# Products of x blocks 2 and 3 of the last block joined into one 128x4608 instruction, block 0's third spectra summed at once, and a new order

## Chip, cores and metric

One Trainium2 chip, one of its cores. The time is device microseconds of one launch. The kernel before has been timed three times: 206.28, 206.78 and 206.79 us, median 206.78.

## What is computed

Two independent results stand side by side in the output of 1 x 2048 x 1152 bfloat16 numbers. Cut to what matters:

```python
# A: local attention, 32 heads of 18, window of 8 keys at distance 0, 2, .. 14 behind the query
qkv = A_x @ A_wqkv                      # 2048x576 @ 576x1728
logits[s, w] = q[s] . k[s - 2*w] * 18**-0.5      # -1e9 where s - 2*w < 0
o[s] = sum_w softmax(logits)[s, w] * v[s - 2*w]
a = o @ A_wo                            # 2048x576 @ 576x576

# B: short convolution, product, long convolution, gate
k_shift = sum_t k[s - t] * shift_k[:, t]         # 4 taps
kv = k_shift * v
y = irfft(rfft(kv, 4096) * rfft(ssm_k, 4096))[:2048] + kv * ssm_D
b = q * y
out = concat(a, b)
```

## The kernel before, in words

**Work units.** The kernel is written as 361 small jobs with names. A table of names at the top, `ORDER`, is walked once at the end (L1103 before the change), and each job emits its instructions in that order to the five engines' queues. There is no scheduler behind it: each engine executes its own instructions in the order in which the table emits them, and semaphores hold an instruction until what it reads is there and what it overwrites has been read. So the table alone decides what stands behind what in each queue.

**Part A.** `q..`, `k..`, `v..` are the projections (L317 and L433, matmuls at L322, L326, L333 and, for the first pieces, L439): for example `k13a` and `k13b` are the two halves of tokens 1024 to 2047 of column group 3 of k, 8 matmuls of 512 columns and two small tails on TensorE, then one copy by ScalarE out of PSUM (L355). `Lhgc` multiplies q by shifted k (VectorE, L706), `Ghgc` sums the product over each head on TensorE (L720). `sm0a` to `sm0d` are the softmax of token half 0: maximum and difference on VectorE (L744 to L748), exponential on ScalarE (L752), sum on TensorE with logarithm and power on ScalarE (L763, L764), scaling on VectorE (L756). `D` spreads the weights over partitions by DMA, `V` multiplies them with v (VectorE, L813), `A` adds eight terms on TensorE (L824, L838), `O` is the output projection (L888, L880).

**Part B.** The tokens fall into four blocks of 512. `Ti` makes kv of block i from the taps on VectorE (L517, L520, L536). `Mi0` and `Mi1` fold kv (L545 on TensorE, two copies by ScalarE at L548). `xigh` transforms block i to spectra (L682, one copy at L684), three parts of 2304 numbers for each of 128 partitions, in the tile `xw`. `Fm` folds filter block m (L602, two copies at L605), `Kmcg` transforms it (L567 and L568, one copy at L618) into the tile `Ks`; eight `K` units for each of four blocks. The spectra are held as part 0, part 1 and their sum; the sum is the "third spectrum", so that a complex product takes three real ones. For blocks 2 and 3 the sum is made by DMA (`Tx`, `Tk`), for blocks 0 and 1 on VectorE: `ak` for the filter and `ax` for x (L942). `U` adds filter blocks by DMA. `RG0` to `RG4` are ScalarE copies that regroup the weights of v (L780).

**The products.** For output block j, third t of the columns and x block i, `pjti` multiplies three parts of the spectrum of x block i by that of filter block j-i, one VectorE instruction of 128x2304 (`spectral_product`, L950). `zjti` adds it into PSUM, 16 matmuls (L975), and the last i copies the result out by ScalarE (L988); for the last one, (3,2,3), half is copied by VectorE. In the last output block, j = 3, the products of x blocks 0 and 2 are subtracted first (`y3t0`, L958), so that only `z3t0`, `z3t1` and `z3t3` exist. `i` is the inverse transform (L1010), `b` folds back (L1059), `g` gates with q (L1075) and stores; `i3384L` and `g3384` are the same for the last 192 columns (L1029, L1038, L1020) and end the kernel.

**What holds a unit back.** PSUM is handed out as four tiles of two banks in turn (`banks`): a unit on TensorE that needs a tile waits until ScalarE has copied the unit that used it four tiles earlier. `M` and `F` take two tiles each, `K`, `x` and `G` groups one. A product is written to one of five homes (`PRODUCT`, by the list `PHOMES`); it waits until the `z` that read the home before has run. Homes 2 and 3 lie side by side in `qk`, 2304 numbers each.

Of the kernel before, what the change touches and what calls it, by code (L numbers as in the profile page):

```python
# [12 lines left out]
ALU = mybir.AluOpType  # L13
# [7 lines left out]
    T0 k03a' T1 S1 k03b I1 k02a k02b Lk2 Lv2 I0 k00a' Lk3 Lv3 M01 X5 k00b q10a Ex q10b Lf3 T2 Lo3 q13a' q13b  # L21
    k10a k10b T3 k13a' Lf2 k13b q12a q12b N2 Lo2 k01a M10 k01b Lf1 M00 k11a k11b q11a M11 q11b Lf0 N3 Lw SV L001
    k12a M20 k12b x001 M21 x021 q24a x020 q24b x000 Lo1 k24a Fr Lo0 Z2 N1 RG3 k24b RG2 F3 RG0 F2 L000 K310 G000
    K311 K210 K211 L002 K313 G001 RG4 F1 G002 L003 G003 K302 L004 G004 K301 L010 K212 L011 K303 K213 K203 N0 F0
    L012 K200 K300 G010 L013 K201 K312 K202 RG1 G011 G012 K113 K103 G013 L014 G014 K112 K102 K101 L100 K100 K010
    K111 K110 sm0a K001 K013 sm0b v24a' L101 v24b L102 G100 L103 G101 K012 sm0c sm0d U3 U2 K000 K011 K003 G102
    K002 D0 D1 v11a v11b G103 L104 G104 ak00 M30 v12a' v12b ak02 v01a ak01 L110 G110 M31 L111 G111 v01b v00a'
    L112 G112 L113 Wl v00b G113 x031 U1 L114 G114 V04 v10a' v10b A04 sm1a sm1b v02a v02b v03a' sm1c v03b x201
    V10 V11 sm1d V12 A10 v13a' v13b D2 x330 x310 x301 V13 A11 V20 V21 x200 x331 x230 x010 x221 A20 x321 V22 x210
    x011 V23 D3 V34 ax02 x220 x030 x300 D4 A21 V40 V41 A34 D5 O000' x211 V42 x320 x231 x111 x131 Tx2 A40 V43  # L30
    x120 x101 ax00 x130 ax01 V50 x121 x311 O001 A41 V51 O100' p000 x100 x110 O010 A50 V52 z000 O011' V53 O101
    A51 Tk2 p010 z010 ax10 O020' O021 p020 z020 O110' ak10 i000 p200 i02880 Q0 p100 z100 p101 p110 p111 Q1 z101
    i02881 i001 p121 p120 O111 z110 p201 z111 z120 p210 z121 O120 p211 z200 z210 z211 p212 z212 z201 p202 z202
    Tx3 p220 Tk3 p221 O030' p222 O121 b0288 z220 p301 z221 O031' p302 b00 z222 p303 i200 i100 g0 Q2 p300 y300
    p312 i12880 i201 i101 i12881 z300 z301 z303 p310 p311 y310 O130 b10 b1288 p313 g1 Q3 p322 O131' z310 p320
# [1100 lines left out]
```

## Time and profile before

| | us |
|---|---|
| median of three runs | 206.78 |
| the profiled execution | 206.3 |
| its span, first to last instruction | 204.6 |
| what lies around the span | 1.7 |
| busy: TensorE, VectorE, ScalarE | 196.9, 192.3, 155.6 |
| last product of the last block done on VectorE | 195.85 |
| last matmul issued | 199.6 |

A line of the timeline gives start, duration, engine, source line, operation, out<-in, the number of instructions merged, and in brackets how long the engine sat idle and who released it. PE is TensorE, PEld its weight load, DVE VectorE, ACT ScalarE. Instructions of one engine overlap a little: what counts for the rate is the distance from one start to the next, not the duration.

### The profile page before, as it was taken

The page shows a single profiled execution, that of the slowest core. Times are in us where ns is not written, and L with a number is a line of the kernel's source. Part 1 is how long each engine was busy: PE and PEld are TensorE (multiplying, and loading weights), DVE is VectorE, ACT ScalarE, POOL GpSimd, SP SyncE. Part 2 cuts the span into 40 slices and gives each one's busy share as a digit, 9 for nine tenths or more (in the row PEclk, how much of TensorE's full clock was granted, in tenths as well). Part 3 has the DMA queues.
Part 4 walks back from the last instruction along what each step waited for, and adds up shares of the span by engine and source line. Part 5 has one row for each costly group of instructions (what it writes and reads, how often), then busy time and mean ns, then how long its engine had stood idle before and what let it go on. Part 6 is the DMA issues. An engine that isn't in the chain of part 4 may idle for free.

```text
span 204.6 us, 5004 instructions
## 1 busy us (share of the span) xinstructions
PE 196.9 (96%) x2074; PEld 109.9 (54%) x2074; DVE 192.3 (94%) x146; ACT 155.6 (76%) x223; POOL 60.8 (30%) x106
## 2 busy tenths in 40 slices
PE   7999999999989999999999999999999999999990
PEld 2543544334455646543245556776666767766660
DVE  7559999999999999999999999999999999899992
ACT  4788995678899999966578678886778767767760
POOL 8989500011348581400380000004090001030300
PEclk9999999999999999999999999999999999999997
DMA  6999899989509869999899990879989303944555
GB/s 197 280 293 306 175 289 373 214 177 281 169 3 146 111 82 185 167 180 222 157 235 216 248 244 34 141 183 334 186 227 233 100 28 122 227 130 145 153 182 150
DMA packets 34916, 38.48 MB, mean 188 GB/s; under 512 B 17523, under 2 KB 28911, under 8 KB 34894
## 3 DMA queue, kind: packets, MB, share of 16 engines
q1 hardware_dynamic: 26668, 24.29, 46.5%
q0 software_dynamic: 5760, 11.36, 29.5%
q10 hardware_dynamic: 2466, 2.51, 3.6%
q8 instruction: 16, 0.26, 0.5%
q14 instruction: 6, 0.05, 0.1%
HBM read 13.11 MB, written 4.72 MB: 87 GB/s over the span
## 4 chain that ended last, share of the span: by engine, by line
PE 88%; DMA 3%; ACT 2%; DVE 2%; issue 1%; SPq 1%; DVEq 0%
PE ps_proj L322 18%; PE ps_fx L682 8%; PE ps_wo L888 8%; PE ps_z L975 8%; PE ps_inv L1010 7%; PE ps_acc L824 7%; PE ps_fk L567 5%; PE ps_log L720 5%; DMA Ks<-in_A_x_dram 3%; PE ps_proj L333 3%; PE ps_proj L326 3%; PE ps_proj L439 3%; PE ps_fk L568 3%; PE ps_fold L545 2%; PE ps_wo L880 1%
## 5 line engine op out<-in xcount | busy, mean ns | idle before, releaser
L322 PE MATMUL ps_proj<-xw 128*128 128x512 bf16 x160 | 38.5, 380 | 0.0
L706 DVE TENSOR_TENSOR av<-qk 128x4096 bf16<-128x4096 bf16 (+1 forms) x16 | 31.7, 2014 | 0.1
L322 PEld LDWEIGHTS <-xw 128*128 128x128 bf16 x160 | 13.9, 98 | 19.4 <-issue 5.7
L988 ACT ACTIVATE av<-ps_z 128x768 bf16<-128x768 f32 x23 | 17.2, 811 | 6.5 <-PE ps_z L975 6.0
L517 DVE TENSOR_TENSOR tB<-kj,skb 128x4608 bf16<-128x4608 bf16 (+1 forms) x8 | 19.3, 2416 | 0.1
L950 DVE TENSOR_TENSOR qk<-xw,Ks 128x2304 bf16<-128x2304 bf16 x14 | 18.9, 1354 | 0.3 <-PE ps_z L975 0.3
L684 ACT ACTIVATE xw<-ps_fx 128x576 bf16<-128x576 f32 x32 | 18.6, 665 | 0.3 <-PE ps_fx L682 0.2
L618 ACT ACTIVATE Ks<-ps_fk 128x576 bf16<-128x576 f32 x32 | 18.6, 699 | 0.2 <-PE ps_fk L568 0.2
L355 ACT ACTIVATE qk<-ps_proj 128x1024 bf16<-128x1024 f32 x14 | 14.3, 1023 | 5.2 <-PE ps_proj L333 2.8
L888 PE MATMUL ps_wo<-qk 128*128 128x288 bf16 x128 | 17.9, 287 | 0.0
L626 POOL DMA_DIRECT2D Ks<-Ks x8 | 10.1, 1426 | 26.0 <-PE ps_back L1059 19.3
L682 PE MATMUL ps_fx<-xw,TB 128*128 128x288 bf16 x128 | 17.7, 287 | 0.0
L567 PE MATMUL ps_fk<-Ks,TB 128*128 128x384 bf16 x62 | 16.5, 327 | 0.1
L824 PE MATMUL ps_acc<-av,ident 64*64 64x512 bf16 x160 | 15.3, 378 | 0.0
L1010 PE MATMUL ps_inv<-av,TI 128*128 128x288 bf16 (+1 forms) x112 | 15.2, 292 | 0.0
L568 PE MATMUL ps_fk<-Ks,TB 128*128 128x192 bf16 x62 | 15.2, 246 | 0.0
L682 PEld LDWEIGHTS <-TB 128*128 128x128 bf16 x128 | 11.9, 98 | 5.9 <-issue 2.7
L888 PEld LDWEIGHTS <-qk 128*128 128x128 bf16 x128 | 11.7, 98 | 5.4 <-issue 2.7
L355 ACT ACTIVATE v<-ps_proj 128x1024 bf16<-128x1024 f32 x9 | 9.3, 1033 | 6.5 <-PE ps_proj L322 4.5
L813 DVE TENSOR_TENSOR av<-Ks,v 128x4096 bf16<-128x4096 bf16 x6 | 13.5, 2286 | 0.0
L827 ACT ACTIVATE qk<-ps_acc 128x1024 bf16<-128x1024 f32 x8 | 8.2, 1024 | 6.7 <-PE ps_acc L824 6.7
L1010 PEld LDWEIGHTS <-TI 128*128 128x128 bf16 x112 | 10.6, 98 | 4.2 <-issue 1.1
(195 smaller groups left out, 441.6 us busy)
## 6 DMA issues: line engine op xcount, KB each, us to landing
Ks<-Ks POOLq DMA_DIRECT2D x8, 576.0 KB, 7.8
TB<-av SPq DMA_DIRECT2D x12, 256.0 KB, 5.4
kj<-in_B_k_dram SPq DMA_DIRECT2D x6, 504.0 KB, 7.0
vt<-in_B_v_dram SPq DMA_DIRECT2D x8, 288.0 KB, 5.3
Ks<-av SPq DMA_DIRECT2D x8, 256.0 KB, 5.6
out_dram<-qk ACTq DMA_DIRECT2D x5, 288.0 KB, 3.7
Ks<-in_A_x_dram SPq DMA_DIRECT2D x2, 576.0 KB, 5.4
xw<-in_A_wqkv_dram SPq DMA_DIRECT2D x2, 576.0 KB, 6.2
```

What stands on the lines that cost most here:

```text
L322: nc.tensor.matmul(ps[:, jp, :], wq(kb, comp, 128 * ct, 128), xT(kb, 1024 * jj + 512 * jp, 512), **se)
L355: nc.scalar.activation(view(t, o + pad + 1024 * jj, [[512, 2], [1, 512]]), ps[:], ACT.Copy)
L517: tt(to, view(kj, row * D, [[D, n], [D, 4], [1, D]]), view(skb, row * D, [[D, n], [0, 4], [1, D]]), ALU.mult)
L567: nc.tensor.matmul(o[:, 0:2], w, rhs[:, 0:2], start=start, stop=stop)
L568: nc.tensor.matmul(o[:, 2], w, rhs[:, 2], start=start, stop=stop)
L618: nc.scalar.activation(view(Ks, k_at(m, cs ^ (m & 1)) + 96 * gi, [[768, 3], [384, 2], [1, 96]]), acc3(ps), ACT.Copy, scale=(PSG, MSG)[cs][ ...
L682: nc.tensor.matmul(ps[:, pm, 0:HD], TX[:, 2 * pm + c, 128 * gi:128 * gi + 128], kv[:, 2 * c + pm, HD * h:HD * h + HD], start=(c == 0), sto ...
L706: tt(view(P, at, [[step, 4], [256, nj], [1, 256]]), view(t, o + 256 * hh, [[0, 4], [512, nj], [1, 256]]), view(tk, ok + 2 + 8 * ug + 256 * ...
L824: nc.tensor.matmul(acc[64 * o:64 * o + 64, h, :], ident[64 * h:64 * h + 64, 64 * h:64 * h + 64], view(P[s], 256 * u, [[2048, 2], [1, 256]] ...
L888: nc.tensor.matmul(ps[:, r, 0:HD], oT(hh, j + 2 * r, t)[:, o:o + 128], wo[:, t // 2, t % 2, HD * h:HD * h + HD], start=(t == 0 and not fli ...
L950: tt(product_home(n), view(xw, HB * XG[i] + QTR * t, [[HB, 3], [1, QTR]]), view(Ks, k_at(j - i, 0) + QTR * t, [[HB, 3], [1, QTR]]), ALU.mult)
L1010: nc.tensor.matmul(ps[:, c, 0:n], TI[:, sl, pm, 128 * c:128 * c + 128], Yall(j % 2, pm, sl, slice(c0, c0 + n)), start=(pm == 0 and sl == 0 ...
```

## The change

Three things change; the five engines do the same arithmetic.

1. For j = 3 the products of x blocks 2 and 3 become one instruction, `two_products`, of 128x4608, written over homes 2 and 3 at once. The three jobs `p303`, `p313`, `p323` go; `p302`, `p312`, `p322` do both.
2. The sums for block 0 (`ak00`, `ak01`, `ak02` and `ax00`, `ax01`, `ax02`, 128x768 each) become one `ak00` and one `ax00` of 128x2304.
3. `ORDER` is a new table throughout.

```diff
-    def third_sum(t, at, w):
+    def third_sum(t, at):
-        a, b, c = (view(t, at + HB * part, [[1, w]]) for part in range(3))
+        a, b, c = (view(t, at + HB * part, [[1, HB]]) for part in range(3))
         tt(c, a, b, ALU.add)
+    def two_products(n):
+        j, t, i = todo[n]
+        home, at = PRODUCT[PHOMES[n]]
+        assert (PHOMES[n], PHOMES[n + 1], XG[i + 1] - XG[i]) == (2, 3, 3)
+        tt(view(qk, at, [[HB, 2], [QTR, 3], [1, QTR]]), view(xw, HB * XG[i] + QTR * t, [[3 * HB, 2], [HB, 3], [1, QTR]]),
+           view(Ks, k_at(j - i, 0) + QTR * t, [[3 * HB, 2], [HB, 3], [1, QTR]]), ALU.mult)
...
     for n, (j, t, i) in enumerate(todo):
-        job(f"p{j}{t}{i}", spectral_product, n)
+        if (j, i) != (NBL - 1, 3):
+            job(f"p{j}{t}{i}", two_products if (j, i) == (NBL - 1, 2) else spectral_product, n)
...
-    for t in range(3):
-        job(f"ak0{t}", third_sum, Ks, k_at(0, 0) + QTR * t, QTR)
-        job(f"ax0{t}", third_sum, xw, HB * XG[0] + QTR * t, QTR)
-    job("ak10", third_sum, Ks, k_at(1, 0), HB)
-    job("ax10", third_sum, xw, HB * XG[1], HB)
+    for j in range(2):
+        job(f"ak{j}0", third_sum, Ks, k_at(j, 0))
+        job(f"ax{j}0", third_sum, xw, HB * XG[j])
```

Of the table, the two ends of block j = 3:

```diff
-    p311 y310 O130 b10 b1288 p313 g1 Q3 p322 O131' z310 p320 z311 p321 z313 ... y320 p323 ... g2 z320 z321 z323 b30 i3384L
+    p311 O131 i22880 y310 z310 z311 z313 i300 g1 p320 i22881 i301 Q3 p322 b2288 y320 z320 p321 z321 g2 z323 b30 i3384L
```

The queues of SyncE are the same instructions in the same order; on GpSimd one small DMA (L358) moves ahead of two memsets (L367, L369). The order is told at three places. The first is ScalarE's queue where the folds of kv end and the filter stage begins: L548 are the pairs of copies of `M`, L355 those of projections, L684 those of `x`, L780 the first `RG`. Before, from the copies of `M11` on:

```order
L548 ACTIVATE xw<-ps_fold 128x576 x2
L355 ACTIVATE qk<-ps_proj 128x1024
L548 ACTIVATE xw<-ps_fold 128x576 x2
L355 ACTIVATE qk<-ps_proj 128x1024
L684 ACTIVATE xw<-ps_fx 128x2x3x96
L548 ACTIVATE xw<-ps_fold 128x576 x2
L684 ACTIVATE xw<-ps_fx 128x2x3x96 x2
L355 ACTIVATE qk<-ps_proj 128x1024
L684 ACTIVATE xw<-ps_fx 128x2x3x96
L780 ACTIVATE xw<-Ks 128x576
```

The same place after, from the copies of `M10` on:

```order
L548 ACTIVATE xw<-ps_fold 128x576 x2
L684 ACTIVATE xw<-ps_fx 128x2x3x96
L548 ACTIVATE xw<-ps_fold 128x576 x6
L684 ACTIVATE xw<-ps_fx 128x2x3x96
L355 ACTIVATE qk<-ps_proj 128x1024
L684 ACTIVATE xw<-ps_fx 128x2x3x96
L780 ACTIVATE xw<-Ks 128x576
```

The pairs of `M11`, `M20` and `M21`, which had other copies between them, now follow each other, and one `x` unit (`x021`) has left this place for a later one.

The second place is the end of the filter stage in ScalarE's queue, from the last `G` of the first half of the logits (L724) to the next copy of v: L618 are `K` units, L752 is the exponential `sm0b`, L763 and L764 belong to `sm0c`. Before:

```order
L724 ACTIVATE av<-ps_log 128x1024
L618 ACTIVATE Ks<-ps_fk 128x6x96 x9
L752 ACTIVATE av<-av 128x2048
L355 ACTIVATE v<-ps_proj 128x1024
L618 ACTIVATE Ks<-ps_fk 128x6x96
L763 ACTIVATE av<-ps_tot 128x256
L764 ACTIVATE av<-av 128x256
L618 ACTIVATE Ks<-ps_fk 128x6x96 x4
```

After:

```order
L724 ACTIVATE av<-ps_log 128x1024
L618 ACTIVATE Ks<-ps_fk 128x6x96 x6
L752 ACTIVATE av<-av 128x2048
L618 ACTIVATE Ks<-ps_fk 128x6x96 x2
L355 ACTIVATE v<-ps_proj 128x1024
L618 ACTIVATE Ks<-ps_fk 128x6x96
L763 ACTIVATE av<-ps_tot 128x256
L764 ACTIVATE av<-av 128x256
L618 ACTIVATE Ks<-ps_fk 128x6x96 x6
```

The exponential stands three `K` units further ahead; of the 32 `K` units 18 stood ahead of this piece before, and 17 do now.

The third place is the end of VectorE's queue, from the gate of block 1 on: L950 and L958 are products of 2304, L953 the joined ones, the rows `av<-av,qk` the subtractions `y`, the rows `TB<-v,TB` the gates. Before:

```order
L1075 TENSOR_TENSOR TB<-v,TB 128x2304
L950 TENSOR_TENSOR qk<-xw,Ks 128x2304
L950 TENSOR_TENSOR av<-xw,Ks 128x2304
L950 TENSOR_TENSOR v<-xw,Ks 128x2304
L958 TENSOR_TENSOR av<-av,qk 128x2304
L950 TENSOR_TENSOR qk<-xw,Ks 128x2304
L1075 TENSOR_TENSOR TB<-v,TB 128x2304
L986 CAST av<-ps_z 128x4x192
```

These are the gate `g1`, then `p322`, `p320`, `p321`, `y320`, `p323`, the gate `g2` and the last copy. After:

```order
L1083 TENSOR_TENSOR TB<-v,TB 128x2304
L958 TENSOR_TENSOR av<-xw,Ks 128x2304
L953 TENSOR_TENSOR qk<-xw,Ks 128x4608
L966 TENSOR_TENSOR av<-av,qk 128x2304
L958 TENSOR_TENSOR v<-xw,Ks 128x2304
L1083 TENSOR_TENSOR TB<-v,TB 128x2304
L994 CAST av<-ps_z 128x4x192
```

The last product ahead of the end is now `p321` in place of `p323`, and the joined product stands ahead of the subtraction.

More of the change, by code (lines that the diff above doesn't have):

```diff
@@ L20 @@
 ORDER = """
[L21 to L35, printed above, removed]
@@ L37 @@
+    z300 z301 z303 p310 p312 b20 i12881 O130' b1288 p311 O131 i22880 y310 z310 z311 z313 i300 g1 p320 i22881
+    i301 Q3 p322 b2288 y320 z320 p321 z321 g2 z323 b30 i3384L g30 g3384
 """
```

15 lines of the change are left out of this document (14 added, 1 removed).

## The prediction

> **What bounds the kernel now.** I read the page first: the busy shares, and the chain of work that ended last, by engine.
>
> ```profile
> PE 196.9 (96%) x2074; PEld 109.9 (54%) x2074; DVE 192.3 (94%) x146; ACT 155.6 (76%) x223; POOL 60.8 (30%) x106
> PE 88%; DMA 3%; ACT 2%; DVE 2%; issue 1%; SPq 1%; DVEq 0%
> ```
>
> TensorE is busy 96% of the span and carries 88% of the chain; VectorE is close behind with 94%. No engine gets less arithmetic by this change. So only three things can move the end: TensorE's idle gaps, the time that it loses in passing from one kind of matmul to another, and VectorE or ScalarE running late enough to make new gaps. Where each engine is full is told by the windows (busy time of PE, PEld, DVE, ACT, POOL in each stretch, then the granted clock):
>
> ```profile
> 46.00:56.00 10.00, 10.00 (x82) 4.34 (x81) 9.72 (x9) 8.42 (x12) 2.52 (x6) 1.00 0.90 231
> 60.00:70.00 10.00, 9.59 (x93) 5.45 (x94) 10.00 (x6) 9.95 (x17) 8.63 (x9) 1.00 0.82 113
> 70.00:80.00 10.00, 10.00 (x100) 5.98 (x99) 9.86 (x11) 10.00 (x18) 5.48 (x5) 1.00 0.81 120
> 80.00:90.00 10.00, 10.00 (x91) 5.33 (x88) 10.00 (x7) 9.02 (x15) 2.38 (x2) 1.00 0.99 174
> 90.00:140.00 50.00, 50.00 (x543) 26.92 (x541) 49.78 (x32) 36.74 (x52) 6.42 (x9) 1.00 0.85 196
> ```
>
> From 60 to 80 us, the filter stage, ScalarE is as full as TensorE (9.95 and 10.00 of 10): it copies 32 `K` units out of PSUM, and TensorE can be no more than four PSUM tiles ahead of it. Before and after that stage ScalarE has room (8.42 of 10; 36.74 of 50). The granted clock is 1.00 in all of them, so I leave it out. Last, the waits of TensorE and of its weight loads (in total, times, longest):
>
> ```profile
> PE ps_log L720 <- DVE av L706: 0.6, 1, 0.6
> PE ps_z L975 <- DVE Ks L950: 0.2, 1, 0.2
> PEld L975 <- DVE av L958: 0.8, 3, 0.3
> ```
>
> Behind the start there is little to win: 0.6 at the first `G` (60.4 us) and 1.0 at the `z`.
>
> **The instructions that are joined.** VectorE loses seven instructions: three products and four sums. What one costs is the distance of starts, not the duration:
>
> ```profile
> 190.70 1.35 DVE L950 TENSOR_TENSOR av<-xw,Ks 128x2304 bf16<-128x2304 bf16 x1
> 191.97 1.35 DVE L950 TENSOR_TENSOR v<-xw,Ks 128x2304 bf16<-128x2304 bf16 x1
> 48.34 2.56 DVE L517 TENSOR_TENSOR tB<-kj,skb 128x4608 bf16<-128x4608 bf16 x1
> 50.93 2.75 DVE L520 TENSOR_TENSOR xw<-xw,tB 128x2304 bf16<-128x2304 bf16 x2
> 81.04 2.28 DVE L706 TENSOR_TENSOR v<-qk 128x4096 bf16<-128x4096 bf16 x1
> 83.24 2.28 DVE L706 TENSOR_TENSOR av<-qk 128x4096 bf16<-128x4096 bf16 x1
> L942 DVE TENSOR_TENSOR Ks<-Ks 128x768 bf16<-128x768 bf16 x3 | 1.5, 552 | 0.0
> L942 DVE TENSOR_TENSOR Ks<-Ks 128x2304 bf16<-128x2304 bf16 x1 | 1.4, 1352 | 0.0
> ```
>
> Two products of 2304 take 2 x 1.27 = 2.54 us. One of 4608 takes 2.59 by the tap products (48.34 to 50.93), and 2.20 x 4608/4096 = 2.48 by the logits: between 0.06 won and 0.05 lost, times three. I take nothing. Of the sums a duration exceeds the distance by 1.35 - 1.27 = 0.08, so three small ones take 3 x (0.552 - 0.08) = 1.42 and the large one 1.27: 0.15 won, twice, 0.3 in all. By distances VectorE wins 0.1 to 0.5 us, and I take 0.3; by durations it would be 1.0 (3 x (2 x 1.35 - 2.56) + 2 x (3 x 0.552 - 1.352)), the upper bound of this gain. Lying on a path that TensorE sets, it buys nothing by itself. The Trainium skill, "Perfetto Trace Analysis", section "Optimizing Scalar/DVE Operations", puts the access overhead of a VectorE instruction on SBUF at about 60 ns, says that profiled latency is about twice that, and that grouping helps where the engine is saturated; by it seven instructions fewer would be an estimated 0.42 us, inside my bounds.
>
> **Term 1, the folds of kv (about 47 us): +0.7 us on TensorE.** The new table lets `M10`, `x000`, `M11`, `M20`, `M21` and `x020` follow each other. These rows of TensorE and ScalarE give the prices:
>
> ```profile
> 48.40 0.66 PE L682 MATMUL ps_fx<-xw,TB 128*128 128x288 bf16 x4
> 48.99 0.68 PE L545 MATMUL ps_fold<-xw,fold 128*64 128x288 bf16 x8
> 49.61 0.67 PE L682 MATMUL ps_fx<-xw,TB 128*128 128x288 bf16 x4
> 49.43 0.64 ACT L684 ACTIVATE xw<-ps_fx 128x576 bf16<-128x576 f32 x1
> 49.96 1.20 ACT L548 ACTIVATE xw<-ps_fold 128x576 bf16<-128x576 f32 x2
> 51.02 0.68 ACT L684 ACTIVATE xw<-ps_fx 128x576 bf16<-128x576 f32 x1
> ```
>
> On TensorE an `x` takes 0.59 (48.40 to 48.99) and an `M` 0.62 (48.99 to 49.61); on ScalarE 0.53 (49.43 to 49.96) and a pair 1.06 (49.96 to 51.02). Four `M` and one `x` are 3.07 us of TensorE and 4 x 1.06 + 0.53 = 4.77 of ScalarE. An `M` holds two of the four tiles, so `M21` waits for both copies of `M11`, and `x020` and the projection behind it for those of `M20`. ScalarE is 4.77 - 3.07 = 1.7 late at the end of it; the tiles that were free at its start absorb between nothing and 1.1. So TensorE waits 0.6 to 1.7; I take 1.4, near the upper end, since every second unit waits once the tiles are used up. Part of it is not lost, only put off: `x021` (0.59) comes later now. So the first filter fold, `F3`, starts about 0.7 later than here:
>
> ```profile
> 55.89 0.42 PE L602 MATMUL ps_rev<-Ks,flip 128*128 128x288 bf16 x2
> 58.12 1.16 ACT L605 ACTIVATE Ks<-ps_rev 128x576 bf16<-128x576 f32 x2
> 60.36 0.61 PE L720 MATMUL ps_log<-av,E 128*32 128x512 bf16 x8 [0.62 <-DVE av L706]
> ```
>
> and its copies on ScalarE about 0.5 later than 58.12, the rest being room that ScalarE has there.
>
> **The wait at the first `G` goes, and gains nothing.** `L000` stands earlier, so the 0.62 us at 60.36 are gone. But the cover under it, ScalarE, is 9.95 of 10 full from 60 on: the `K` units come no faster than ScalarE copies them. If ScalarE were not the limit, this would be 0.6 us won (first rival).
>
> **Term 2, the end of the filter stage (76 to 89 us): +0.3 on ScalarE, and 1.0 of TensorE's work put off.** The rows of ScalarE and VectorE:
>
> ```profile
> 76.81 1.02 ACT L724 ACTIVATE av<-ps_log 128x1024 bf16<-128x1024 f32 x1
> 77.73 4.99 ACT L618 ACTIVATE Ks<-ps_fk 128x576 bf16<-128x576 f32 x9
> 82.50 2.00 ACT L752 ACTIVATE av<-av 128x2048 bf16<-128x2048 bf16 x1
> 88.56 0.65 ACT L618 ACTIVATE Ks<-ps_fk 128x576 bf16<-128x576 f32 x1 [0.16 <-PE ps_fk L568]
> 75.94 2.27 DVE L706 TENSOR_TENSOR av<-qk 128x4096 bf16<-128x4096 bf16 x1
> 79.89 1.23 DVE L748 TENSOR_TENSOR av<-av 128x2048 bf16<-128x2048 bf16 x1
> ```
>
> The copy of the last `G` (76.81) hangs on VectorE's product of 75.94 and on VectorE, full from 60 to 80, and comes no sooner. Nine `K` then take 82.50 - 77.73 = 4.77, or 0.53 each. After the change six stand there: 77.73 + 6 x 0.53 = 80.9. The exponential needs the softmax's difference (79.89 + 1.23 = 81.1), so ScalarE waits about 0.3, with nine `K` queued behind it and TensorE's `K` units behind their tiles. The last `K` copy thus comes 0.5 + 0.3 = 0.8 later than 88.56, less up to 0.4 of slack that ScalarE has in that stretch (9.02 of 10 busy): +0.4 to +0.9. By then TensorE has also done less of everything else than before: `x021` (0.59), and five fewer changes of the kind of matmul (55 against 60, counted in the order), which must still come. One such change costs:
>
> ```profile
> 40.50 1.90 PE L322 MATMUL ps_proj<-xw 128*128 128x512 bf16 x8
> 42.33 0.39 PE L333 MATMUL ps_proj<-xw 64*128 64x512 bf16 x2
> 42.65 1.04 PE L322 MATMUL ps_proj<-xw 128*128 128x512 bf16 x4
> 43.62 0.68 PE L545 MATMUL ps_fold<-xw,fold 128*64 128x288 bf16 x8
> ```
>
> Eight matmuls in one piece take 1.83 (40.50 to 42.33), twice four take 2 x 0.97 = 1.94: 0.1 a change, 0.5 for five, and with `x021` 1.0 to 1.1, taken as 1.0. So at the last filter unit the new kernel is 0.4 to 0.9 plus 1.0, that is 1.4 to 1.9, behind.
>
> **Between 90 and 168 us: nothing.** TensorE is at 50.00 of 50 and I count the same number of changes over the whole program, so it passes the lag on, neither more nor less.
>
> **Term 3, waits that the lag fills: -0.7.** Of the 1.0 us at the `z` I let 0.7 go, because VectorE, which does not lag by the same, gets ahead of TensorE. Bounds: 0 and 1.0.
>
> **Term 4, the tail: +0.6.** Its prices:
>
> ```profile
> 187.03 2.14 PE ps_z L975 x48
> 189.18 2.39 PE ps_inv L1010 x16
> 191.56 0.37 PE ps_back L1059 x8
> ```
>
> The joined `p322` overwrites homes 2 and 3, so it waits for `z313`, and behind it in VectorE's queue stand `y320` and `p321`. From the end of `z313` VectorE needs 2.56 + 1.27 + 1.35 = 5.2 us until `p321` is there. TensorE has three inverse units (x8 each, 2.39/2 = 1.2), one fold (0.37) and `z320` (2.14/3 = 0.71): 4.7. With 0.1 to release it, it waits 0.6 for `z321`. Before the change one more inverse and fold stood there, and `p321` was written before `y320`. The bounds are 0, should `p322` find home 3 free early enough, and 0.9 by 2.7 for the joined product and the whole distance of 1.35 for `y320`.
>
> **Sum.** 1.4 to 1.9, less 0.7, plus 0.6: 1.3 to 1.8, and I take +1.6 on the profiled execution of 206.3 us: **207.9 us**. The median shown lies 0.5 above that execution, so a median after could come out that much higher; I stay with the sum.
>
> **The rivals.**
>
> *VectorE is the pace-setter (faster).* It is 49.78 of 50 full from 90 to 140, and its 10.00 in 60 to 70 says that the logits, not the `K` copies, may set the filter stage's end. Then the burst of `M` is absorbed, starting VectorE's logits earlier pays, and the waits of 0.6 and 1.0 go, with 0.3 of VectorE's instructions; the 0.6 of the tail stays: 206.3 - 1.9 + 0.6 = 205.0, and with 0.2 of the burst left 205.2. Against it: TensorE shows no wait at all on VectorE between 61 and 167 us.
>
> *No change, about 206.5.* The burst costs 0.6 by its lower bound, and the gap at 60.36 gives 0.6 back.
>
> *The homes push through (slower, 209.0).* The joined product holds two homes, so `p302` waits for `z222` instead of `z221`; VectorE then idles some 1.1 us (a `z` of 0.71 and its release) and TensorE has no more in hand at the last block than VectorE has lead. That is 207.9 + 1.1. It decides where VectorE reaches `p302` with `z222` still to come and its next `z` within a product of TensorE. The Trainium skill speaks for it in the section named: where an engine that isn't saturated causes bubbles on others, breaking instructions up may complete the work sooner; the join does the opposite. Against it is the inverse work of block 2 that stands ahead of `z300`.
>
> **How the numbers follow.** The forecast has 0.42, the third rival 0.10, no change 0.20, faster 0.28. Runs of this kernel differ by 0.25% (206.28 to 206.79), so 0.3%, or 0.6 us, is about what a measurement can tell. The range runs from the first rival's 205.2 to the third's 209.0, and the forecast's own from 207.3 to 208.6.
>
> **What would show it.** The steps are right if TensorE shows waits on ScalarE's copies of L548 near 48 to 51 us that sum to 0.6 to 1.7, if `F3`'s copies start near 58.6, if ScalarE waits for VectorE at the exponential near 81 us, if the last `K` copy lies between 89.0 and 89.5, and if `z321` waits on VectorE 0.6 in the tail. The prediction is wrong if the last `K` copy lies at or before 88.6, or if TensorE gains more than 0.7 between 90 us and the last block.

## The result: 209.2 us, 1.3% slower

The changed kernel takes 209.2 us (median of 4 runs, 208.69 to 209.63) where the kernel before takes 206.78; the ratio is 1.0127, with an interval of 1.0103 to 1.0151. The forecast had the direction, and 207.9 us with an upper bound of 209.0, so the loss is 2.4 to 2.6 us where 1.6 was forecast. Left out below are two of the four executions of one later run, `first_folds_early`, with a granted clock of 0.85 (the profiled one, whose profile is therefore not read) and 0.91, and one of the five of `fill`, which took 498 us.

The page of the changed kernel, busy shares:

```profile
PE 199.6 (96%) x2074; PEld 111.6 (54%) x2074; DVE 192.4 (93%) x139; ACT 155.1 (75%) x223; POOL 64.1 (31%) x106
```

VectorE has its seven instructions fewer and the same busy time. TensorE's busy time grows by 2.7 us with no matmul more: short waits between matmuls of one group are counted in it, so from here on I read starts and not busy times.

**A common zero.** The two profiled executions differ by 0.76 us before TensorE's first matmul that the table of names could have moved. The last matmul of the first projections (L441) starts here in the kernel before, and behind it in the changed kernel:

```profile
18.00 0.38 PE L441 MATMUL ps_proj<-xw 64*128 64x512 bf16 x1
```

```profile
18.76 0.38 PE L441 MATMUL ps_proj<-xw 64*128 64x512 bf16 x1
```

From that matmul to the end of the span it is 204.55 - 18.00 = 186.55 us before and 207.92 - 18.76 = 189.16 after: **2.61 us** more. No kernel was profiled twice, so the scatter of this figure itself is not known; but four kernels that share their order up to `z212` (changed, `single`, `fill`, `both`) agree there within 0.05 us on each milestone below, much closer than the runs' times, so I use it beside the ratios. Counted from the same zero, the changed kernel is late by this much (start of the first and end of the last copy of a filter unit on ScalarE, starts of `z212` and `z320` on TensorE):

| | zero to end, us | first K copy | last K copy | z212 | z320 |
|---|---|---|---|---|---|
| before | 186.55 | 0 | 0 | 0 | 0 |
| changed | +2.61 | +0.94 | +1.06 | +0.89 | +2.51 |

About 1 us is lost before the filter units begin. `z212` seems to say that this is passed on unchanged for 100 us, but it misleads: in both kernels it waits for VectorE's product `p212`, and by then the kernel before has done the output unit `O120` (1.23 us), for which the changed one has done only `b00` (0.35). The first inverse unit behind `z222` (`i200` before, `i100` in the changed kernel) is a place at which both have done the same units on TensorE:

```profile
175.87 6.05 PE L1010 MATMUL ps_inv<-av,TI 128*128 128x288 bf16 x48
```

```profile
178.37 5.07 PE L1018 MATMUL ps_inv<-av,TI 128*128 128x288 bf16 x40
```

There the changed kernel is (178.37 - 18.76) - (175.87 - 18.00) = **1.74 us** late, and the last 0.87 are lost behind it, in the tail. The windows of the changed kernel that answer to those of before:

```profile
46.00:56.00 10.00, 9.38 (x78) 4.54 (x78) 9.83 (x8) 8.58 (x15) 1.99 (x3) 1.00 0.79 210
60.00:70.00 10.00, 9.31 (x90) 5.10 (x89) 8.92 (x6) 10.00 (x16) 8.09 (x9) 1.00 0.67 92
80.00:90.00 10.00, 10.00 (x97) 5.83 (x95) 9.90 (x9) 9.62 (x16) 2.38 (x2) 1.00 1.02 179
90.00:140.00 50.00, 50.00 (x526) 27.16 (x527) 49.14 (x28) 37.35 (x54) 6.01 (x8) 1.00 0.85 188
```

TensorE now has gaps at the folds of kv (9.38 of 10 where it had 10.00), VectorE idles in 60 to 70 us (8.92), and ScalarE is fuller to 90 us (9.62 where it had room with 9.02). In the rows of the folds and of `F3` on TensorE, the three folds `M11`, `M20`, `M21` take 52.02 - 48.79 = 3.23 us, where three at 0.62 take 1.86:

```profile
48.79 3.12 PE L545 MATMUL ps_fold<-xw,fold 128*64 128x288 bf16 x24
52.02 0.65 PE L682 MATMUL ps_fx<-xw,TB 128*128 128x288 bf16 x4
57.57 0.42 PE L602 MATMUL ps_rev<-Ks,flip 128*128 128x288 bf16 x2
```

So 1.37 us of waits stand there. And the tail, VectorE first, then TensorE. Rows: `p302` joined, `p310`, `p312` joined, `p311`, `p322` joined, `p321`; then the end of `z313`, the inverse units behind it, and `z321`:

```profile
175.82 2.56 DVE L953 TENSOR_TENSOR qk<-xw,Ks 128x4608 bf16<-128x4608 bf16 x1 [1.15 <-PE ps_z L983]
...
184.52 1.36 DVE L958 TENSOR_TENSOR av<-xw,Ks 128x2304 bf16<-128x2304 bf16 x1 [0.95 <-PE ps_z L983]
185.82 2.56 DVE L953 TENSOR_TENSOR qk<-xw,Ks 128x4608 bf16<-128x4608 bf16 x1
188.30 1.35 DVE L958 TENSOR_TENSOR v<-xw,Ks 128x2304 bf16<-128x2304 bf16 x1
...
193.37 2.55 DVE L953 TENSOR_TENSOR qk<-xw,Ks 128x4608 bf16<-128x4608 bf16 x1
...
197.24 1.35 DVE L958 TENSOR_TENSOR v<-xw,Ks 128x2304 bf16<-128x2304 bf16 x1
```

```profile
192.97 0.33 PE L983 MATMUL ps_z<-qk,identn 64*64 64x384 bf16 x4
193.89 3.82 PE L1018 MATMUL ps_inv<-av,TI 128*128 128x384 bf16 x24 [0.59 <-ACT av L996]
...
198.64 0.36 PE L983 MATMUL ps_z<-v,identn 64*64 64x384 bf16 x4
```

VectorE idles 1.15 us in front of `p302` and 0.95 in front of `p310`. TensorE waits 0.59 us, not at `z321` but at `i300`, for ScalarE's copy of `z313`; and `z321` starts 0.05 us behind `p321` (197.24 + 1.35 = 198.59).

### The profile page after: what moved, and what is told of

It reads as the page before. It is cut to its first block, busy times and chain, and to the rows that moved or that the text cites. A ratio compares the mean times of both kernels' runs of the same rounds, so it can differ in the third digit from the quotient of the medians.

```text
span 207.9 us, 4997 instructions
## 1 busy us (share of the span) xinstructions
PE 199.6 (96%) x2074; PEld 111.6 (54%) x2074; DVE 192.4 (93%) x139; ACT 155.1 (75%) x223; POOL 64.1 (31%) x106
## 3 DMA queue, kind: packets, MB, share of 16 engines
q10 hardware_dynamic: 2466, 2.51, 3.5%
## 4 chain that ended last, share of the span: by engine, by line
PE 66%; ACT 3%; issue 1%; DVE 0%; DVEq 0%; ACTq 0%
PE ps_z L983 9%; PE ps_wo L888 8%; PE ps_inv L1018 7%; PE ps_fx L682 7%; PE ps_acc L824 7%; PE ps_proj L322 7%; PE ps_fk L567 5%; PE ps_log L720 4%; PE ps_fk L568 2%; PE ps_wo L880 1%; PE ps_proj L333 1%; ACT Ks L605 1%; PE ps_acc L838 1%; PE ps_proj L326 1%; PE ps_back L1067 1%; PE ps_tot L762 1%
## 5 line engine op out<-in xcount | busy, mean ns | idle before, releaser
L355 ACT ACTIVATE qk<-ps_proj 128x1024 bf16<-128x1024 f32 x14 | 14.0, 1025 | 9.0 <-PE ps_proj L333 5.6
L618 ACT ACTIVATE Ks<-ps_fk 128x576 bf16<-128x576 f32 x32 | 19.0, 701 | 0.2 <-PE ps_fk L568 0.2
L684 ACT ACTIVATE xw<-ps_fx 128x576 bf16<-128x576 f32 x32 | 18.9, 662 | 0.1
L1018 PE MATMUL ps_inv<-av,TI 128*128 128x288 bf16 (+1 forms) x112 | 15.8, 292 | 0.6 <-ACT av L996 0.6
L355 ACT ACTIVATE v<-ps_proj 128x1024 bf16<-128x1024 f32 x9 | 9.2, 1024 | 7.5 <-PE ps_proj L333 4.7
L1021 ACT ACTIVATE v<-ps_inv 128x576 bf16<-128x576 f32 (+1 forms) x14 | 9.5, 680 | 4.4 <-PE ps_inv L1018 4.4
```

What stands on the lines that cost most here:

```text
L355: nc.scalar.activation(view(t, o + pad + 1024 * jj, [[512, 2], [1, 512]]), ps[:], ACT.Copy)
L618: nc.scalar.activation(view(Ks, k_at(m, cs ^ (m & 1)) + 96 * gi, [[768, 3], [384, 2], [1, 96]]), acc3(ps), ACT.Copy, scale=(PSG, MSG)[cs][ ...
L684: nc.scalar.activation(view(xw, HB * XG[i] + 96 * gi + 1152 * h, [[HB, 2], [384, 3], [1, 96]]), view(ps, 0, [[512, 2], [96, 3], [1, 96]]), ...
L1018: nc.tensor.matmul(ps[:, c, 0:n], TI[:, sl, pm, 128 * c:128 * c + 128], Yall(j % 2, pm, sl, slice(c0, c0 + n)), start=(pm == 0 and sl == 0 ...
```

## Experiments

Each ran beside the kernel before on the same chip. "Zero to end" is the figure above, against 186.55 us.

| run | ratio to before, interval | zero to end | first K copy | last K copy | z212 | z320 |
|---|---|---|---|---|---|---|
| changed kernel | 1.0127, 1.0103 to 1.0151 | +2.61 | +0.94 | +1.06 | +0.89 | +2.51 |
| spread | 1.0117, 1.0089 to 1.0145 | +2.49 | +0.71 | +0.93 | +0.76 | +2.38 |
| burst | 1.0033, 1.0016 to 1.0049 | +0.55 | +0.53 | +0.55 | +0.57 | +0.55 |
| joins | 1.0191, 1.0167 to 1.0215 | +4.06 | -0.01 | 0.00 | +0.02 | +3.97 |
| joins_after_reader | 1.0205, 1.0167 to 1.0243 | +4.51 | -0.01 | +0.04 | +0.05 | +4.41 |
| sums | 1.0016, 1.0000 to 1.0032 | +0.21 | +0.04 | +0.02 | +0.28 | +0.21 |
| single | 1.0111, 1.0094 to 1.0129 | +2.66 | +0.94 | +1.11 | +0.94 | +2.55 |
| fill | 1.0140, 1.0120 to 1.0161 | +2.81 | +0.93 | +1.10 | +0.94 | +2.71 |
| both | 1.0104, 1.0081 to 1.0126 | +1.78 | +0.94 | +1.11 | +0.94 | +1.68 |
| head90 | 1.0073, 1.0056 to 1.0090 | +1.52 | +0.01 | +0.02 | -0.23 | +1.39 |
| single_fill_head90 | 1.0035, 1.0016 to 1.0054 | +0.60 | -0.02 | +0.03 | -0.22 | +0.51 |
| head | 1.0140, 1.0111 to 1.0168 | +2.62 | +1.18 | +1.32 | +0.89 | +2.51 |
| head_rg_behind | 1.0135, 1.0112 to 1.0159 | +2.54 | +1.16 | +1.25 | +0.81 | +2.43 |
| copies_first | 1.0011, 0.9996 to 1.0025 | +0.14 | -0.02 | +0.16 | +0.17 | +0.13 |
| first_folds_early | 1.0143, 1.0113 to 1.0172 | | | | | |
| folds_early_tail | 1.0088, 1.0066 to 1.0110 | +1.43 | +0.59 | +0.72 | +0.60 | +1.34 |
| x_units_early | 1.0056, 1.0035 to 1.0078 | +0.76 | +0.83 | +0.85 | +0.86 | +0.66 |
| pairs_first | 1.0078, 1.0054 to 1.0102 | +1.40 | +0.56 | +0.74 | +0.58 | +1.32 |
| pairs_and_folds | 1.0060, 1.0041 to 1.0079 | +1.02 | +0.18 | +0.37 | +0.20 | +0.94 |

### The folds of kv: spread and burst

`spread` is the changed kernel with the folds drawn apart, `burst` the kernel before with them bunched:

```diff
 spread, in the changed order
-M10 L001 x000 Lo2 M11 M20 M21 Lf1 Lo1 x020 Lf0 q24a q24b x001
+M10 L001 x000 Lo2 M11 x001 q24a q24b M20 Lf1 Lo1 M21 Lf0 x020
 burst, in the order of before
-q11a M11 q11b Lf0 N3 Lw SV L001 k12a M20 k12b x001 M21 x021 q24a x020 q24b x000
+q11a q11b Lf0 N3 Lw SV L001 k12a k12b x001 M11 M20 M21 x021 x020 q24a q24b x000
```

> The changed kernel with the folds of kv drawn apart: M10, x000, M11, x001, then the projection q24, then M20, M21 and x020. Nothing else of it is moved. My theory (the burst of copies costs TensorE 1.7 us that nothing later gives back): the three waits of the changed kernel at M20, M21 and x020 (0.57, 0.59, 0.50 us) go, the last copy of a filter unit comes about 1.5 us earlier, and the ratio to the kernel before falls from 1.0127 to about 1.005 (207.8 us beside 206.8). Rival (the filter stage is paced by ScalarE and VectorE, whenever TensorE gets there): the folds start the stage earlier but the last filter copy stays within 0.4 us of where it is, and the ratio stays at 1.011 or above.

> The kernel before with only the folds of kv bunched: M11, M20, M21 follow each other and the x units come behind them; the instructions are those of before. My theory: TensorE waits 1.2 to 1.7 us there, the filter stage ends as much later, and VectorE falls behind by the same, so the later wait of TensorE at z212 (0.34 us in the kernel before) stays at 0.2 or more; ratio 1.006 to 1.009. The prediction's term 3 as rival (VectorE does not lag by the same, so later waits fill): the waits at the z go to under 0.1 and the ratio is 1.003 to 1.005. Second rival (absorbed by the filter stage): ratio under 1.002.

`spread` gave back 0.12 us of the 1.7 that I expected, and the first filter copy came 0.23 us earlier: the rival's numbers came out. But the waits did not go as expected, so it is a weak test of them. `M11` takes 48.83 - 47.77 = 1.06 us, `M20` and `M21` together 53.34 - 51.60 = 1.74, where one takes 0.62 without a wait: 0.94 of the 1.37 us are still there.

```profile
47.77 0.95 PE L545 MATMUL ps_fold<-xw,fold 128*64 128x288 bf16 x8
48.83 0.65 PE L682 MATMUL ps_fx<-xw,TB 128*128 128x288 bf16 x4
...
51.60 0.93 PE L545 MATMUL ps_fold<-xw,fold 128*64 128x288 bf16 x12
...
53.34 0.65 PE L682 MATMUL ps_fx<-xw,TB 128*128 128x288 bf16 x4
```

In `burst` the folds and what TensorE waits for at the `z` read:

```profile
47.29 2.65 PE L545 MATMUL ps_fold<-xw,fold 128*64 128x288 bf16 x24
50.05 1.19 PE L682 MATMUL ps_fx<-xw,TB 128*128 128x288 bf16 x8
```

```profile
PE ps_z L975 <- DVE Ks L950: 0.2, 1, 0.2
PEld L975 <- DVE av L958: 0.8, 3, 0.3
```

Three folds take 2.76 us, so 0.9 us of waits arise here, and the kernel ends 0.55 us later (with six passages fewer between kinds of matmul, that is changes of their tile shape: 116 against 122, worth 0.6 by the prediction's price). The ratio lies in term 3's bracket, below mine. But its mechanism is refuted: TensorE is 0.57 us late at `z212`, and the waits at the `z` are to the digit those of the kernel before. A lag does not fill them.

### The joins and the sums in the old order

`joins` and `joins_after_reader` put only the joined products into the kernel before, `sums` only the joined sums:

```diff
 joins_after_reader (joins has p302 ahead of b00 z222)
-p302 b00 z222 p303 i200 ... y300 p312 i12880 ... z303 p310 p311 y310 ... b1288 p313 g1 Q3 p322 O131'
+b00 z222 p302 i200 ... y300 i12880 ... z303 p310 p312 p311 y310 ... b1288 g1 Q3 O131'
-z310 p320 z311 p321 z313 ... b20 y320 p323 i22881
+z310 p320 z311 z313 p322 ... b20 y320 p321 i22881
 sums
-ak00 M30 ... ak02 v01a ak01 ... ax02 x220 ... ax00 x130 ax01
+M30 ... v01a ak00 ... x220 ... x130 ax00
```

> The kernel before with only the three joined products of x blocks 2 and 3, in its own order; in VectorE's queue they stand where the changed kernel has them. My theory: a joined product overwrites two homes, so it waits for the later reader, and it has to end before the subtraction that a single product of block 3 could follow; VectorE idles about 1 us at each of p302 and p310, and the tail is 0.4 to 1.2 us longer: ratio 1.002 to 1.006. Rival (three instructions fewer on an engine that is 94% busy help): ratio 0.997 to 1.000.

> The kernel before with only the three joined products, as in the first try, but with p302 behind z222 in the table. (In the first try p302 stood ahead of it, so it overwrote p222's product and z222 added p303's in its place, and had to wait for p302: 1.9 us of that run were due to this.) Theory (a joined product waits for the later of two readers; VectorE idles where single products of the next block filled the time): VectorE idles 1 us or more before p302 and 0.7 us or more before p310, z300 and z310 wait for y300 and y310 by 2 us or more together, ratio 1.009 to 1.015. Rival (the join itself costs nothing, only the flaw did): ratio 1.004 or below.

> The kernel before with only the sums for block 0 joined (four instructions fewer on VectorE), at the place of the last of the three. My theory: 0.3 us of VectorE less on a path that TensorE sets: ratio 0.999 to 1.001. Rival (VectorE is the pace-setter between 90 and 168 us): 0.3 us or more won, ratio 0.9985 or below.

The sums win nothing. In `joins`, `z222` waits 1.71 us for `p302`, which stands ahead of it and overwrites the product that it was to add; `joins_after_reader` is without this flaw. It still costs 4.5 us in the profiled execution of the old order, far more than in the changed one, whose whole tail loses 0.87. The rows of `joins_after_reader`, VectorE's `p302` and `p310`, then TensorE's `z310` and the window behind it:

```profile
176.58 2.56 DVE L953 TENSOR_TENSOR qk<-xw,Ks 128x4608 bf16<-128x4608 bf16 x1 [1.52 <-PE ps_z L983]
184.02 1.36 DVE L958 TENSOR_TENSOR av<-xw,Ks 128x2304 bf16<-128x2304 bf16 x1 [0.95 <-PE ps_z L983]
```

```profile
190.47 0.36 PE L983 MATMUL ps_z<-av,ident 64*64 64x384 bf16 x4 [2.17 <-DVE av L966]
```

```profile
191.00:195.00 4.00, 4.00 (x47) 2.23 (x40) 2.84 (x3) 1.51 (x2) 0.51 (x1) 0.57 0.52 148
```

VectorE has nothing to do while it waits for the second home, and TensorE then waits 2.17 us for the subtraction; behind that wait the granted clock is 0.57 for 4 us, which makes part of the 4.5. Of six runs five had a mean granted clock of 0.987 to 0.989 and took 210.59 to 211.47 us; the sixth had 0.998 and took 208.87, which is 1.012 of the median before. So the joins themselves cost about 2.5 us, inside my bracket of 1.009 to 1.015, as far as that one run shows; `joins` less the wait of `z222` says much the same (4.06 - 1.71 = 2.35). In the changed order inverse and output units stand under the wait, and TensorE has no wait at `z300` or `z310`. The Trainium skill, "Perfetto Trace Analysis", section "Optimizing Scalar/DVE Operations", says that breaking instructions up may let work complete sooner where an engine that is not saturated causes bubbles on others. The trace agrees: with the product whole, VectorE sits idle 1.52 and 0.95 us here, and TensorE 2.17.

### The tail of the changed kernel: single, fill, both

```diff
 single, in the changed order
-p302 p301 ... y300 z300 ... z303 p310 p312 b20 ... y310 z310 z311 z313 i300 g1 p320 i22881
+p302 p301 p303 ... y300 p312 z300 ... z303 p310 b20 ... y310 p313 z310 z311 z313 i300 g1 p322 p320 p321 i22881
-Q3 p322 b2288 y320 z320 p321 z321
+Q3 b2288 y320 p323 z320 z321
 fill
-O131 i22880 y310 z310 z311 z313 i300
+O131 y310 z310 z311 z313 i22880 i300
```

> The changed kernel with single products of x blocks 2 and 3 in the last block, standing in VectorE's queue as in the kernel before (p301, p303; y300, p312, p310, p311, y310, p313, g1, p322, p320, p321, y320, p323); TensorE's order is untouched. In the changed kernel VectorE idles 1.15 us at p302 (for z222) and 0.95 us at p310 (for z300); z321 starts 0.05 us behind p321's end, and i300 waits 0.59 us for ScalarE's copy of z313. Theory A (two limits of equal height: i300's wait for the copy takes up just the time by which VectorE is late for z321): freeing VectorE alone leaves the copy's wait, so ratio 1.011 to 1.013. Rival B (the join alone is what the tail loses): z313 comes earlier as well and 0.6 us or more are won, ratio 1.010 or below.

> The changed kernel with one inverse unit, i22880, moved from before z310 to between z313 and i300, so that TensorE has 1.15 us of work while ScalarE copies z313. Theory A: i300's wait of 0.59 us goes, but z310 then waits for y310 (190.92 us in the changed kernel) and z321 for p321, both as late as before on VectorE, so nothing is won: ratio 1.012 to 1.013. Rival C (the copy behind z313 is the whole loss of the tail): 0.6 us won, ratio 1.010 or below.

> The changed kernel with single products and with i22880 behind z313, the two edits together. Theory A: only together they win, 0.6 us, ratio 1.0095 to 1.0105. Rival: what either wins alone and no more.

Zero to end changes by +0.05, +0.20 and **-0.83 us**: neither edit alone wins, both together do, as theory A has it. The ratios do not separate them (1.0111, 1.0140, 1.0104, with intervals that overlap), so this rests on one profiled execution of each. The same two edits behind the long head, below, bear it out by the ratios: 1.0035 against 1.0073, or 0.8 us. In `fill` the wait at `i300` is gone and stands at `z310` instead, for VectorE's subtraction:

```profile
190.16 0.36 PE L983 MATMUL ps_z<-av,ident 64*64 64x384 bf16 x4 [0.83 <-DVE av L966]
```

In `both` VectorE idles 0.50 us at `p302` where it idled 1.15, and the inverse units run through behind `z313`:

```profile
174.23 1.36 DVE L958 TENSOR_TENSOR qk<-xw,Ks 128x2304 bf16<-128x2304 bf16 x1 [0.50 <-PE ps_z L983]
```

```profile
191.08 4.81 PE L1018 MATMUL ps_inv<-av,TI 128*128 128x288 bf16 x32
```

### The head: head90, head, and what was tried on it

`head90` and `head` take the order of before up to `D1` and up to `F3`, and the rest from the changed one. `single_fill_head90` has the tail's two edits behind the long head; `head_rg_behind` is `head` with `F3 L000 L002 RG4 F2 RG1 K310` for `F3 L000 L002 RG1 RG4 F2 K310`.

> The order of the kernel before up to the end of the filter stage (its first 90 us, to the second spreading of the weights), and behind it the order of the changed kernel with its joined products and sums; what stood earlier or later across the seam is done once. Drawing the folds of kv apart gave back almost nothing, so the first 90 us are in question. Theory D (the head as a whole carries the 1.4 to 1.9 us that were forecast for the last filter unit): ratio 1.003 to 1.005, that is 1.6 us less than the changed kernel. Rival E (what the head loses would come back behind it, and the loss lies in the last two blocks, where VectorE waits for z222 and z300): ratio 1.010 or above.

> Head of the kernel before up to 90 us, and behind it the changed order with single products and with i22880 behind z313. Theory (the losses of head and tail lie behind one another on TensorE, so they add): the 1.1 us and the 0.8 us by which these lowered the profiled span, counted from the end of the first projections, come off together: ratio 1.002 to 1.005. Rival (one hides the other): ratio 1.007 or above.

> The order of the kernel before up to the first filter fold F3 (its first 57 us), and the changed kernel behind it; TensorE passes between kinds of matmul three times more than in either (125 against 122, 0.1 us each). Theory D (of the head's 1.1 us, the waits at the folds M20, M21 and x020 are all): the three waits go, 1.66 us, the waits where the filter stage begins stay between 1.0 and 1.5 us, and with 0.3 us for the passages the ratio is about that of the longer head, 1.006 to 1.008. Rival (the rest of the first 90 us carries it, the folds do not): ratio 1.011 or above.

> The head of the kernel before up to F3 as before, but with the regrouping copy RG1 behind the copies of F2. Theory G: ScalarE reaches the copies of F2 1.2 us earlier than in the first such head, the 1.58 us wait at K210 falls to about 0.4, and the ratio is that of the long head, 1.006 to 1.009. Rival (the head up to F3 holds no loss): 1.012 or above.

The long head wins 1.09 us, and 1.18 on top of the tail's edits: head and tail add. The first and last filter copies are back at 0.01 and 0.02. What the long head leaves does not arise at its seam. At the `x` unit behind `G113` (`x031` before, `x010` in `head90`), where both have done the same units, `head90` is (101.78 - 18.52) - (101.34 - 18.00) = 0.08 us early; at the inverse unit behind `z222` it is (177.02 - 18.52) - (175.87 - 18.00) = 0.63 late, with no tail yet. So some 0.6 us belong to the new order of the middle, from 101 to 176 us. It makes 40 passages there where the order of before has 36; at 0.1 us that would be 0.4. No run tests it by itself. The short heads won nothing, though TensorE's waits at the folds went. The row of `head`'s ScalarE between the copies of `F3` and `F2`, and what TensorE waited for (the lines of these kernels stand one lower):

```profile
59.63 2.44 ACT L779 ACTIVATE xw<-Ks 128x576 bf16<-128x576 bf16 x2
```

```profile
PE ps_fk L566 <- ACT Ks L604: 1.5, 1, 1.5
```

At the seam one regrouping copy more stands ahead of the first filter copy; moving it behind `F2`'s copies only put it ahead of the filter units' own (+1.16). Both are poor tests of the folds, and good ones of something else: TensorE's 1.37 us at the folds can go without any gain, as long as ScalarE reaches the filter units no earlier.

### Is it the wait at the first G? copies_first

```diff
 in the order of before
-SV L001 ... RG2 F3 RG0 F2 L000 K310 G000
+SV L000 ... RG2 F3 F2 RG0 L001 K310 G000
```

> The kernel before with two small changes of order and no other: ScalarE's regrouping copy RG0 behind the copies of the filter fold F2, where it stood between those of F3 and F2; and the logits product L000 ahead of L001. TensorE's order stays. In the kernel before TensorE waits 0.93 us at G000 and 0.13 us at K311, and where L000 came early (the changed kernel, the two heads) the wait only moved on to the filter units. Theory F (that wait is ScalarE's: the filter units wait for the copies of F2 behind RG0): both waits go and the kernel is 0.6 to 1.0 us faster than before, ratio 0.995 to 0.997. Rival (ScalarE is full to 89 us, so what is won at 60 us is lost by then): ratio 0.998 to 1.001.

The wait at `G000` went and came back at `K211`, behind two more filter units, now for a filter copy of ScalarE:

```profile
61.84 0.32 PE L567 MATMUL ps_fk<-Ks,TB 128*128 128x384 bf16 x1 [0.74 <-ACT Ks L618]
```

The ratio of 1.0011 holds no gain, as the rival says.

### Where ScalarE falls behind

```diff
 folds_early_tail: both, and (first_folds_early: the changed kernel, and)
-q12b k13a' Lf2 N2 k12a k12b k13b M01 q13a' q13b M10 L001
+q12b M01 k13a' Lf2 N2 k12a k12b M10 k13b q13a' q13b L001
 pairs_first: both, and
-k02a' I0 T0 Lk2 k03a' T1 k00a' S1 k01a k01b k03b Lv2 Lk3 k00b X5 T2 q12a M00 k02b Lv3 ... Ex I1 Lf3
+k02a' k02b T0 Lk2 I0 k03a' T1 S1 k03b I1 k00a' Lv2 Lk3 k00b k01a k01b X5 T2 q12a M00 Lv3 ... Ex Lf3
 pairs_and_folds: pairs_first, with M01 behind k00b and M10 behind k12b
 x_units_early, in the order of before
-k11b q11a M11 q11b ... k12a M20 k12b x001 M21 x021 q24a x020 q24b x000 Lo1
+k11b x000 q11a M11 q11b ... k12a x001 M20 k12b M21 x021 q24a x020 q24b Lo1
```

> The changed kernel with the folds M01 and M10 moved up, M01 behind q12b and M10 behind k12b, where ScalarE idles 2.15 us (before 43.96 us); the passages between kinds of matmul stay 122. Theory G (ScalarE is the pace of the stage from 45 us to the last filter unit, and what it copies late is late at the end): the first copy of a filter unit and the last one come 0.8 to 1.1 us earlier, counted from the end of the first projections, and the ratio falls to 1.007 to 1.009. Rival (the distance of the folds M11, M20, M21, x020 is what counts, and they stay together): ratio 1.011 or above.

> The changed kernel with M01 and M10 moved up as in first_folds_early, and with single products and i22880 behind z313 as in both. Theory G: the two gains add, 1.0 us and 0.8 us off the changed kernel's 209.4 us behind the first projections, ratio 1.003 to 1.006. Rival: one of the two gains is lost, 1.008 or above.

> The kernel before with two units moved up, x000 behind k11b and x001 behind k12a, into the time before 48 us in which ScalarE has gaps of 0.5 us and more; 120 passages in place of 122. Theory G: ScalarE reaches the copies of F2 up to 1.0 us earlier, TensorE's waits at G000 and K311 (1.06 us) shrink, and the kernel is 0.4 to 1.0 us faster than before, ratio 0.995 to 0.998. Rival (TensorE sets the stage's pace, the waits move on as they did with the regrouping copy): ratio 0.999 to 1.001.

> The changed kernel with the tail's two edits (single products, i22880 behind z313), and with the first projections finished pair by pair (k02a k02b, k03a k03b, k00a k00b, k01a k01b) and the transposes I1 behind the second pair; all folds stay late. 118 passages between kinds of matmul where the kernel with the tail's two edits has 120. Theory H (ScalarE falls behind by idling there): its idle of 2.5 us behind the first projections goes and the first copy of a filter unit comes 0.3 us earlier or more; 0.3 to 0.8 us less than with the tail's edits alone (188.55 us behind the first projections), ratio 1.005 to 1.008. Rival (it only idles later, since the folds come late): first filter copy within 0.2 us, ratio 1.009 or above.

> The same with M01 behind k00b, where the kernel before has it, and M10 behind k12b. Theory H: ScalarE is as far as in the kernel before when the filter stage begins; first filter copy 0.6 to 1.0 us earlier than in the changed kernel, the whole 0.8 to 1.2 us less than with the tail's edits alone, ratio 1.003 to 1.006. Rival: no more than the 0.35 us that the early folds won by themselves, ratio 1.0075 or above.

The windows of the 12 us behind the zero, each in its own fence: before, changed, `pairs_first`, `pairs_and_folds`. The fourth pair of numbers is ScalarE:

```profile
18.00:30.00 12.00, 12.00 (x97) 5.39 (x95) 11.79 (x8) 11.11 (x17) 5.29 (x11) 1.00 1.08 227
```

```profile
18.76:30.76 12.00, 12.00 (x81) 4.91 (x79) 11.79 (x8) 8.61 (x13) 7.66 (x18) 1.00 1.07 207
```

```profile
18.59:30.59 12.00, 11.79 (x93) 5.26 (x93) 11.79 (x8) 9.46 (x14) 7.87 (x18) 1.00 1.05 235
```

```profile
18.54:30.54 12.00, 11.79 (x94) 5.19 (x95) 11.79 (x8) 10.25 (x15) 7.96 (x18) 1.00 1.08 226
```

TensorE (12.00 and 11.79) and VectorE (11.79) are about as full in all of them; ScalarE copies for 11.11, 8.61, 9.46 and 10.25 us, and the first filter copy is late by 0, 0.94, 0.56 and 0.18 us. The two edits add: beside `both` (+1.78) the early folds win 0.35 (1.0 was expected), the pairs 0.38, and both 0.76. The folds' 0.35 comes without any passage fewer; of the pairs' 0.38, two passages fewer (118 against 120) may be 0.2, so for the pairs alone theory H is not proven. In `pairs_and_folds` the waits at the folds are nearly all there still (three folds take 51.07 - 48.20 = 2.87 us, 1.0 more than without waits), and yet the filter units begin only 0.18 late:

```profile
48.20 2.75 PE L545 MATMUL ps_fold<-xw,fold 128*64 128x288 bf16 x24
51.07 0.65 PE L682 MATMUL ps_fx<-xw,TB 128*128 128x288 bf16 x4
```

`first_folds_early` by itself showed no gain, on two runs. `x_units_early` came out as neither of its two theories: the copy of `x000` held a PSUM tile that the projection behind it needed, and TensorE waited 0.85 us at 44 us, earlier than any wait it was to remove.

```profile
44.08 0.82 PE L322 MATMUL ps_proj<-xw 128*128 128x512 bf16 x3 [0.85 <-ACT xw L684]
```

No version was faster than the kernel before; `copies_first` (1.0011) is the nearest.

## Why the prediction was right in sign and too small

- **The bound** held: TensorE paces the kernel, no arithmetic went, and VectorE's fewer instructions bought nothing (`sums` 1.0016). The joined product takes 2.48 us of VectorE (185.82 to 188.30 us in the changed kernel), the low bound of 2.48 to 2.59.
- **Term 1** had the right size on TensorE (1.37 us of waits, 1.4 forecast; `F3` starts 0.92 later, 0.7 forecast), but its reason is only a part. I gave the loss to the folds' standing close together. Bunched in the old order they do cost 0.55 us (`burst`). In the new order the waits do not decide: with all of them gone the loss stayed (`head`), and with 1.0 us of them kept most of it went (`pairs_and_folds`). What carries it on is how far ScalarE is with its copies when the filter units begin (+0.94 us), and a good part of that arises 20 us earlier, in its idle time behind the first projections, which I had not looked at.
- **The G wait** "gains nothing" held (`copies_first`).
- **Term 2**: the last filter copy is 1.06 us later, where 0.4 to 0.9 was forecast. The wait at the exponential, of which I made 0.3, is 0.14 (six filter copies end at 82.15 us, it starts at 82.29; rows below).
- **The middle** held as a sum: 1.4 to 1.9 us behind was forecast with the work put off, and at the inverse unit behind `z222` it is 1.74. Some 0.6 of that is what the new order of the middle costs (`head90`), for which I had counted five put-off changes of the kind of matmul as 0.5.
- **Term 3 failed, and with it the size.** "Of the 1.0 us at the z I let 0.7 go, because VectorE, which does not lag by the same, gets ahead of TensorE." Nothing went: the 1.74 us stand at the inverse unit behind `z222`, and the tail comes on top. There were two errors. First, VectorE does lag by the same: `p212` starts 167.82 - 166.17 - 0.76 = 0.89 us later, exactly as `z212` does (rows below). `burst` shows it cleanly: 0.57 us of lag, and the waits of 0.2 and 0.8 us unchanged. A product waits until the `z` that read its home has run (before, VectorE waits 0.21 us at 162.24 and 0.33 at 169.13 for one), so it cannot run ahead of TensorE. Second, the 0.8 was for the most part no wait: it is three gaps of weight loads, 0.24, 0.31 and 0.25 us, and a gap of 0.24 stands in front of `z100` too, which waits for nothing (rows below). Without the -0.7 the sum would have been 2.0 to 2.5, and 208.3 to 208.8 us on the profiled execution.
- **Term 4** was forecast as 0.6 us at `z321`, and is 0.83 (`both` against the changed kernel). From the end of `z313` VectorE needed 5.3 us to finish `p321` (5.2 forecast). But TensorE's wait stood at `i300` for a copy that I had not priced, and hid that `z321` would have waited as long: two limits of equal height, so that removing either one alone gains nothing.
- **The median.** The profiled execution of before lay 0.5 us under the median; I said so and stayed with the sum. That is about the rest of the distance to 209.2.
- **The rivals.** VectorE as pace-setter and no change are refuted. "The homes push through" happened in part: VectorE idles 1.15 and 0.95 us as priced, but in the changed order the work moved under it covers `z300`. In the old order it pushes through (`joins_after_reader`).

The rows for terms 2 and 3: ScalarE's filter copies and the exponential of the changed kernel, then `p212` before and after, then the first weight loads of `z100` and `z300` before.

```profile
78.79 3.36 ACT L618 ACTIVATE Ks<-ps_fk 128x576 bf16<-128x576 f32 x6
82.29 1.91 ACT L752 ACTIVATE av<-av 128x2048 bf16<-128x2048 bf16 x1
```

```profile
166.17 1.36 DVE L950 TENSOR_TENSOR Ks<-xw,Ks 128x2304 bf16<-128x2304 bf16 x1
```

```profile
167.82 1.36 DVE L958 TENSOR_TENSOR Ks<-xw,Ks 128x2304 bf16<-128x2304 bf16 x1
```

```profile
156.74 0.11 PEld L975 LDWEIGHTS <-identn 64*64 64x64 bf16 x4 [0.24 <-issue]
```

```profile
181.85 0.11 PEld L975 LDWEIGHTS <-ident 64*64 64x64 bf16 x4 [0.24 <-DVE av L958]
```

Together: 1.1 us in the head (`head90`), 0.6 in the new order of the middle (what `head90` keeps at the inverse unit) and 0.83 in the tail (`both`) make 2.5 of the 2.61. Open are the 0.6 of the middle, of which the passages would explain 0.4, and 0.3 to 0.4 of the head: early folds and finished pairs recover 0.76, the old head 1.1.

## What to carry to other kernels

Joining two instructions joins their waits: it waits for the later reader and delays what could have run after the first half, so price the two waits before the 0.06 us of overhead. Compare two orders at places where both have done the same work; a milestone in between can hide a part of the loss. When a stage is paced by copies, look for the engine's idle time well ahead of the stage and not only at the waits inside it, since the waits can be removed without gain. Before counting on a lag to fill a later wait, ask whether the producer is held by the consumer; and where a wait sits beside a second limit of the same height, test the two edits together.

## What the runs showed of the hardware

The same 16 transposes at the start (L410) took from 0.84 us (`spread`) to 1.60 (the changed kernel) from the first start to the last, by execution, and the zero, which moves mostly with them, lay anywhere from 17.7 to 18.8 us. Before and after:

```profile
5.03 1.07 PE L410 MATMUL ps_x<-ident,Ks 128*128 128x128 bf16 x16
```

```profile
5.08 1.91 PE L410 MATMUL ps_x<-ident,Ks 128*128 128x128 bf16 x16
```

The granted clock in the windows there is 1.00 in both. The Trainium skill, "TensorE: Matmul & The Clock Gate", section "What you observe", has matmuls at about half rate until some 4 us of sustained work, varying by 0.5 us from run to run; the nearly doubled duration agrees in kind, but the granted clock of the profile does not show it here. And one wait of TensorE of 2.17 us was followed by 4 us at a granted clock of 0.57 (`joins_after_reader`), while behind a wait of the same length at the same place in `joins` the granted clock stayed at 1.00.
